# One more V chunk per batch row held in PSUM, with three units between a row's kept passes and an early drain of V

## The chip, the cores and the metric

The kernel runs on one core of one Trainium2 chip. The metric is the time of one execution on the device in microseconds.

## The reference, cut to what matters

A decode step for 8 batch rows: attention over a cache of 4096 positions, 8 key/value heads of 256 elements and 16 query heads, a small MLP block, and then **the same two again with the same caches and weights**.

```python
x = x + _A_ref(_layernorm(x), k_cache, v_cache, wq, wo)    # first pass over the cache
x = x + _B_ref(_layernorm(x), w1, w2, w3, w4)
x = x + _A_ref(_layernorm(x), k_cache, v_cache, wq, wo)    # second pass, same cache
x = x + _B_ref(_layernorm(x), w1, w2, w3, w4)
```

K and V of one row are 32 chunks of 1 MiB, 512 loads for two passes if nothing is kept. A row's second pass needs the row's x from its first pass: its sums, output projection, MLP and new q, called the row's *chain* below.

## The kernel before

The kernel has 15 slots of 1 MiB in SBUF, the on-chip memory that the loads land in. A *unit* is one pass, one row, one pair of heads: 4 K chunks and 4 V chunks. Each row keeps 11 chunks from its first pass to its second, so 8 x 11 = 88 loads are saved and 424 remain. While 11 slots are occupied, the loads of other units go through the remaining four.

```python
NC = 15
kept = [(GP - 1, kv, n) for n in range(4) for kv in range(2)] + [(GP - 2, 0, n) for n in range(3)]
LAG = 4
# order of units, cut: ps 1 is the second pass, keep = pairs 2 and 3, free = pairs 0 and 1
for b in range(Bn):
    tasks += [(1, b, gp) for gp in keep[::-1]]           # second, kept passes of row b
    if b + 1 < Bn:
        tasks += [(0, b + 1, gp) for gp in keep]         # fills the kept slots again
    ...
    tasks += [(1, b, gp) for gp in free]                 # between here and row b+1's kept
    tasks += [(0, b + 2, gp) for gp in free]             # pass: four units, four slots
# V of a unit trails its K by LAG = 4 chunks: K0' V0 K1' V1 ... , also over the kept passes
```

For each K chunk VectorE transposes the slot twice and TensorE forms scores in 32 matmuls; after four chunks ScalarE takes the exponentials, TensorE transposes P, and 16 matmuls per V chunk sum the outputs. The two passes' small matmuls are spread over the units as generators, one step at a time, evenly over a window:

```python
add_gen("chain", b, chain(b, st), idx + 1, first_of[(1, b), 0] - 1, 30)   # from, until, steps
```

The kernel uses eight PSUM banks of 512 words per partition (PSUM is the memory that matmuls sum into): two for scores, three for outputs, one shared (P transposes, spread q, output transposes), two for the chains' sums.

## Time and profile before

The median of the four runs beside the result was 1153.25 us (1149.37 to 1156.13); the profiled execution spanned 1149.6 us. In lines of the profile PE is TensorE, PEld its weight loads, DVE VectorE, ACT ScalarE, POOL GpSimd and SPq the queue from which the loads are issued; L596 is line 596 of the kernel.

| what | value | how to read it |
|---|---|---|
| moved by DMA | 457.52 MB | at 420 GB/s, the best pace seen, 1089.3 us |
| last load landed | 1133 us | last microsecond at over 40 GB/s |
| loss of pace before that | 43.7 us | 1133 - 1089.3 |
| end after it | 16.6 us | 1149.6 - 1133 |

These last two are the booking: span = MB/0.420 + loss + end, the loads' end known to about 1 us. (Expectations of the experiments add up the loss over slices of ten microseconds instead; that gave 42.0 for before.)

### The profile page before, as it was taken

The page shows a single profiled execution, that of the slowest core. Times are in us where ns is not written, and L with a number is a line of the kernel's source. Part 1 is how long each engine was busy: PE and PEld are TensorE (multiplying, and loading weights), DVE is VectorE, ACT ScalarE, POOL GpSimd, SP SyncE. Part 2 cuts the span into 40 slices and gives each one's busy share as a digit, 9 for nine tenths or more (in the row PEclk, how much of TensorE's full clock was granted, in tenths as well). Part 3 has the DMA queues.
Part 4 walks back from the last instruction along what each step waited for, and adds up shares of the span by engine and source line. Part 5 has one row for each costly group of instructions (what it writes and reads, how often), then busy time and mean ns, then how long its engine had stood idle before and what let it go on. Part 6 is the DMA issues. An engine that isn't in the chain of part 4 may idle for free.

```text
span 1149.6 us, 36707 instructions
## 1 busy us (share of the span) xinstructions
PE 705.3 (61%) x17177; PEld 514.0 (45%) x17177; DVE 548.2 (48%) x904; ACT 113.9 (10%) x234; POOL 15.6 (1%) x25
## 2 busy tenths in 40 slices
PE   3144677457755667456764676646665576647787
PEld 2023455345533455344542454425443365425666
DVE  5145453455354544546254553445534553445352
ACT  0001011100110011001110101010011001100100
POOL 0000000000000000000000000000000000000000
PEclk9999997655655556555565557555575556555655
DMA  9999999999999999999999999999999999999993
GB/s 352 375 420 420 407 385 399 418 412 383 414 420 400 385 399 419 420 403 406 409 420 420 400 400 413 420 420 387 402 412 420 408 371 412 420 410 355 410 420 153
DMA packets 68349, 457.52 MB, mean 398 GB/s; under 512 B 6999, under 2 KB 13030, under 8 KB 13542
## 3 DMA queue, kind: packets, MB, share of 16 engines
q1 hardware_dynamic: 68198, 455.19, 98.0%
q8 instruction: 134, 2.20, 0.8%
q14 instruction: 17, 0.14, 0.0%
HBM read 455.15 MB, written 0.01 MB: 396 GB/s over the span
## 4 chain that ended last, share of the span: by engine, by line
DMA 69%; PE 13%; DVE 11%; SPq 3%; issue 2%; POOL 1%; ACT 0%; POOLq 0%; DVEq 0%; ACTq 0%
DMA slot<-in_A_k_cache_dram 62%; DVE slot L547 9%; DMA slot<-in_A_v_cache_dram 6%; PE sc L555 4%; PE o L596 3%; PE y_ps L318 2%; SPq L148 2%; PE q_ps L274 1%; DMA wq_sb<-in_A_wq_dram 1%; SPq L539 1%; PE o L610 1%; DVE qbd L300 1%; PE o L318 1%; PE h_ps L336 0%; PE misc L381 0%
## 5 line engine op out<-in xcount | busy, mean ns | idle before, releaser
L547 DVE STREAM_TRANSPOSE slot<-slot 128x1024 uint32<-128x1024 uint32 x400 | 472.7, 1222 | 383.7 <-DMA slot<-in_A_k_cache_dram 375.0
L555 PE MATMUL sc<-slot,qbd 128*8 128x128 bf16 x8192 | 280.6, 286 | 345.6 <-DVE slot L547 287.2
L555 PEld LDWEIGHTS <-qbd 128*8 128x8 bf16 x8192 | 194.5, 105 | 430.8 <-issue 298.6
L596 PE MATMUL o<-slot,ptw 128*8 128x256 bf16 x3968 | 242.8, 388 | 55.8 <-DMA slot<-in_A_v_cache_dram 33.9
L564 ACT ACTIVATE p_n<-sc 128x512 bf16<-128x512 f32 x64 | 84.7, 1323 | 780.6 <-PE sc L555 780.6
L596 PEld LDWEIGHTS <-ptw 128*8 128x8 bf16 x3968 | 107.9, 109 | 93.8 <-issue 45.0
L318 PEld LDWEIGHTS <-wo_sb 128*128 128x128 bf16 (+1 forms) x1600 | 64.8, 124 | 16.2 <-issue 15.6
L318 PE MATMUL y_ps<-OT,wo_sb 128*128 128x1 bf16 (+1 forms) x1280 | 55.5, 177 | 1.5 <-issue 1.5
L384 DVE RECIPROCAL rz<-misc 128x8 f32<-128x8 f32 (+1 forms) x33 | 6.4, 193 | 96.3 <-PE misc L381 96.3
L274 PEld LDWEIGHTS <-wq_sb 128*128 128x128 bf16 x1152 | 33.9, 104 | 19.1 <-issue 17.3
L274 PE MATMUL q_ps<-xb,wq_sb 128*128 128x1 bf16 (+1 forms) x1152 | 35.3, 166 | 11.4 <-DMA wq_sb<-in_A_wq_dram 3.6
L584 ACT CAST ptw<-misc 128x128 bf16<-128x128 f32 x64 | 17.5, 274 | 211.9 <-PE misc L577 159.4
L411 PEld LDWEIGHTS misc<-R,o_sb 128*128 128x128 f32 x124 | 25.9, 293 | 11.0 <-issue 11.0
L318 PEld LDWEIGHTS <-w_sb 128*128 128x128 bf16 (+1 forms) x630 | 25.7, 125 | 7.3 <-issue 5.2
L411 PE MATMUL misc<-R,o_sb 128*128 128x8 f32 x124 | 28.8, 343 | 0.0
L232 POOL TENSOR_TENSOR t<-t,nhalf 128x2 f32<-128x2 f32 (+1 forms) x17 | 10.7, 630 | 1075.8 <-DVE t L239 978.0
L318 PE MATMUL y_ps<-HT_t,w_sb 128*128 128x1 bf16 (+1 forms) x560 | 24.2, 177 | 0.5 <-DVE HT_t L359 0.5
L300 DVE TENSOR_SCALAR qbd<-misc,quad 128x64 bf16<-128x64 f32 x64 | 13.8, 278 | 22.0 <-PE misc L294 22.0
L381 PE MATMUL misc<-zm,one 128*128 128x8 f32 (+1 forms) x66 | 18.1, 348 | 6.7 <-ACT ptw L584 6.7
L336 PEld LDWEIGHTS <-w_sb 128*128 128x128 bf16 x560 | 17.2, 105 | 9.6 <-issue 9.2
L336 PE MATMUL h_ps<-xb,w_sb 128*128 128x1 bf16 (+1 forms) x560 | 17.9, 166 | 4.9 <-DVE xb L249 4.6
L381 PEld LDWEIGHTS misc<-zm,one 128*128 128x128 f32 x66 | 15.2, 287 | 11.9 <-ACT ptw L584 8.4
(92 smaller groups left out, 207.7 us busy)
## 6 DMA issues: line engine op xcount, KB each, us to landing
slot<-in_A_v_cache_dram SPq DMA_DIRECT2D x224, 1024.0 KB, 12.3
slot<-in_A_k_cache_dram SPq DMA_DIRECT2D x200, 1024.0 KB, 16.4
wo_sb<-in_A_wo_dram SPq DMA_DIRECT2D x1, 3584.0 KB, 26.6
wq_sb<-in_A_wq_dram SPq DMA_DIRECT2D x3, 1024.0 KB, 7.0
w_sb<-in_B_w_dram SPq DMA_DIRECT2D x1, 1568.0 KB, 12.8
w_sb<-in_B_w_dram SPq DMA_DIRECT2D x3, 448.0 KB, 26.8
wq_sb<-in_A_wq_dram SPq DMA_DIRECT2D x2, 256.0 KB, 10.0
w_sb<-in_B_w_dram SPq DMA_DIRECT2D x2, 112.0 KB, 9.0
```

The lines of the kernel that those rows point to most:

```text
L148: nc.sync.dma_start(t[:, fc * cols : (fc + 1) * cols], src[fc * 128 : fc * 128 + 128, :])
L274: nc.tensor.matmul(q_ps[:, j * Hq + h, :], w, xbs(nb)[:, xi, :], start=(fc == 0), stop=(fc == 3),)
L300: nc.vector.tensor_scalar_mul(qbd[:, :, :, a, :], qs.rearrange("p e (f g u h) -> p (e f) u g h", f=2, u=2, h=2)[:, :, u], quad[:, a : a + 1],)
L318: nc.tensor.matmul(r, w[:, i, lo:hi], rhs(i), start=(first and fc == 0 and i == rows[0]), stop=(stop and i == rows[-1]), skip_group_check= ...
L336: nc.tensor.matmul(h_ps[:, c * nb : c * nb + nb], w, xbs(nb)[:, xi, :], start=(fc == 0), stop=(fc == 3),)
L381: nc.tensor.matmul(z_ps, ones, zm[:], start=True, stop=True)
L411: nc.tensor.matmul(ot_ps[:, j], o_sb[:, 128 * j : 128 * j + 128], R[:], start=True, stop=True)
L547: nc.vector.transpose(w, w)
L555: nc.tensor.matmul(sc[32 * k : 32 * k + 8, 128 * x : 128 * x + 128], qbd[:, ep, gp].rearrange("p a h -> p (a h)"), kv[:, k, 2 * half + e2, ...
L564: nc.scalar.activation(p_sb[:].rearrange("p t i x -> p x t i"), sc[:].rearrange("p (x t i) -> p x t i", x=4, t=4), ACT.Exp, scale=scale_ex ...
L584: nc.scalar.copy(ptw[:, :, :, 6:8], pt_ps.rearrange("p t k (a h) -> p a (t k) h", a=4),)
L596: nc.tensor.matmul(o_ps[32 * q : 32 * q + 8, 256 * (g // 4) : 256 * (g // 4) + 256], ptw[:, a, 4 * (y % 4) + y // 4, w : w + 8], v[:, y * ...
```

## The change

Its intent is to save one more load per row. There is no SBUF slot for it, so a chunk of V goes to PSUM through VectorE, as four 32-bit transposes into four banks ("away"), and returns into the slot of the first kept K chunk ("back"). This takes four of the eight banks, so everything else is packed: one bank for scores, with exponentials in halves; two for outputs; the chain's sums in the shared bank.

```diff
-    LAG = 4
+    inner = (GP - 2, 1, 1)
+    sc = psum.tile([128, 512], FP32, name="sc")
+    o_banks = [psum.tile([128, 512], FP32, name=f"o{n}") for n in range(2)]
+    store = [psum.tile([128, 512], FP32, name=f"store{n}") for n in range(4)]
...                                     # the chain's sums now lie in the bank "misc"
+            early = 0 < b < Bn - 3      # order: a unit of row b ahead of the refill
+            tasks += [(1, b, free[0])] * early + [(0, b + 1, gp) for gp in keep]
+            tasks += [(1, b, gp) for gp in free[early : 1 if b == Bn - 3 else 2]]
...
+    def flushed(n):                     # the V of the unit ahead of a second kept pass
+        ...                             # is used before that pass begins
+        return ps == 1 and gp == keep[-1]
...
+    def away(slot):
+        for n in range(4):
+            nc.vector.transpose(
+                store[n][:].bitcast(U32), slot[:].bitcast(U32)[:, 512 * n : 512 * n + 512]
+            )
```

So it has five parts: the chunk in PSUM (eight loads fewer), its moves, the PSUM layout, the order (in four rows three units instead of four between the refill and the kept pass), and the drain of V, called *flush*.

## The prediction

> **What bounds the kernel now.** I read the page first: its tenths by slice, the DMA queue, the chain that ended last. Then I cut the span into stages with the view of busy time by windows, and read the chain of waits in order of time inside one stage.
>
> ```profile
> span 1149.6 us, 36707 instructions
> PE 705.3 (61%) x17177; PEld 514.0 (45%) x17177; DVE 548.2 (48%) x904; ACT 113.9 (10%) x234; POOL 15.6 (1%) x25
> DMA packets 68349, 457.52 MB, mean 398 GB/s; under 512 B 6999, under 2 KB 13030, under 8 KB 13542
> q1 hardware_dynamic: 68198, 455.19, 98.0%
> DMA 69%; PE 13%; DVE 11%; SPq 3%; issue 2%; POOL 1%; ACT 0%; POOLq 0%; DVEq 0%; ACTq 0%
> slot<-in_A_v_cache_dram SPq DMA_DIRECT2D x224, 1024.0 KB, 12.3
> slot<-in_A_k_cache_dram SPq DMA_DIRECT2D x200, 1024.0 KB, 16.4
> ```
>
> The reader is to see that no engine is above 61% while the DMA queue is busy 98%, and that the cache arrives in 424 loads (224 + 200) of 1024 KB. The number 98% hides something: busy is not the same as fast. By windows (after the engines' busy times: granted clock, DMA share, GB/s):
>
> ```profile
> 225.00:296.00 71.00, 46.62 (x1100) 33.70 (x1101) 34.60 (x65) 5.88 (x15) 1.25 (x2) 0.51 1.00 399
> 296.00:353.00 57.00, 34.60 (x832) 23.71 (x831) 26.96 (x30) 6.93 (x14) 0.00 (x0) 0.58 1.01 420
> 353.00:433.00 80.00, 51.02 (x1231) 37.57 (x1232) 39.91 (x74) 7.16 (x15) 1.25 (x2) 0.51 0.99 393
> 433.00:490.00 57.00, 34.70 (x817) 23.70 (x810) 26.85 (x29) 6.96 (x14) 0.00 (x0) 0.57 1.01 420
> 900.00:960.00 60.00, 41.07 (x1008) 31.07 (x1012) 30.32 (x62) 5.21 (x11) 1.25 (x2) 0.50 0.99 387
> 1018.00:1071.00 53.00, 36.43 (x830) 27.11 (x834) 28.89 (x56) 4.84 (x10) 1.25 (x2) 0.50 0.99 377
> 1132.00:1150.00 18.00, 10.80 (x304) 9.65 (x301) 3.89 (x25) 0.21 (x1) 0.70 (x1) 0.50 0.03 9
> ```
>
> Each row of the batch has a stage at 420 GB/s (kept chunks are used up, 15 slots turn over) and a stage at 377 to 405 (11 slots hold kept chunks, only four turn over, and the row's chain of projections and MLP runs among them). In the chain in order of time the second kind looks like this: a load, two transposes, then the next load, with no queue behind it.
>
> ```profile
> 387.65 8.26 DMA slot<-in_A_k_cache_dram
> 395.93 2.38 DVE slot L547 x2
> 399.00 7.16 DMA slot<-in_A_k_cache_dram
> 406.18 2.37 DVE slot L547 x2
> ```
>
> A slot's turn is thus about 7.2 + 2.4 + 0.6 (scores of the second half) + issue = 11 us for K; four slots at 420 GB/s would allow 4 x 2.50 = 10.0.
>
> With 420 GB/s as the pace, the whole span can be booked. 457.52 MB / 420 = 1089.3 us. What is lost in a window is its length x (1 - rate/420): the first 145 us lose 8.7; the eight stages with a chain lose 3.6, 3.6, 5.1, 2.9, 3.2, 4.1, 4.7 and 5.4 = 32.6; the end (from 1071 us) 18.9, of which 17.6 after the last load. Sum 1149.5 against 1149.6 measured. So every megabyte taken away is worth its 2.4 us only as long as the 32.6 do not grow.
>
> **What the Trainium skill says.** "DMA: Bandwidth & Descriptors", Specifications, gives a fabric ceiling of 435 GB/s and about 358 per core from HBM. The trace agrees with the first (420 held for 57 us) and not with the second. The same page's Rules say that a PSUM access by DMA is not possible, hence the round trip through VectorE here. "PSUM — Partial Sum Buffer", PSUM bank collisions raise a hardware error, says two engines may not touch one bank in the same partitions at the same time, even in different columns. In the built instruction order of the changed kernel I see just that: the first scores into a half of the bank wait for the exponentials of the other half. No run yet shows the cost. "VectorE: DVE Perf Modes", The TRN2 errata, puts a fixed 58 cycles on an SBUF source and 120 on a PSUM source at 0.96 GHz. The trace of before has SBUF transposes only: 1204 ns median for 1024 words, which is 1067 ns of stream plus 137 fixed; so the page's 58 cycles (60 ns) is low here.
>
> **The change part by part.**
>
> Removed: one V load for each of eight rows (the built SyncE stream has 429 entries instead of 437). 8 x 1.0486 MB / 420 = 8 x 2.497 = 20.0 us. All eight fall in the second kept pass, whose loads run in the 420 GB/s stage with a queue, so all of it is on the path.
>
> Added on VectorE: four transposes of 128x512 words to PSUM and four back, per row. Each by my estimate 512/0.96 = 533 ns + 0.14 = 0.67 us, up to 0.75 from PSUM: 64 x 0.7 = 45 us over the kernel, 5.6 per row in two lots of 2.8. "Away" falls where the kept slots are being filled: there VectorE is busy 27 of 57 us and landings are up to 21.4 us after the issue, so eight loads are queued and 2.8 us of VectorE time delay nothing. "Back" falls in the second kept pass, where K needs no transposing and VectorE is idle. I count 0 on the path.
>
> Added on ScalarE: exponentials in 128 halves instead of 64 wholes. Half of 1323 ns plus the 268 ns read of the accumulator is about 0.95 us an instruction; the second accumulator reads cost 64 x 0.27 = 17 us more on an engine that is 10% busy. In the four-slot stage K chunks come 5 us apart, so the wait of the third K's scores for the first exponentials is over before its data lands. In the kept pass it costs about 1 us twice.
>
> Moved (flush): the four V chunks of the last unit are used before the kept K chunks. Four V loads in a row land 2.5 us apart; each use frees a slot for the next four loads. When the last V lands, about 10 us of loads are already issued. The first kept K slot handed on comes after 1.1 (last V) + 1.4 (spreading q) + 2 x 1.2 (two scores) = 4.9 us, later ones every 1.2 to 2.2 us. So the queue should not run dry; cost 0 to 0.5 us per row.
>
> Moved (order): four rows have three units (24 loads) instead of four (32) in the four-slot stage. One might take a quarter off the loss. But before contains three-unit stages already: the windows from 225, 900 and 1018 us lose 3.6, 4.7 and 5.4, mean 4.6; the four-unit ones lose 5.1, 2.9, 3.2 and 4.1, mean 3.8. The loss goes with the chain, not with the number of units, and a denser chain loses slightly more. I book 4 x 0.8 = +3 us.
>
> Moved (PSUM): the chain's sums share the bank of the P transposes and of q, so more waits between PE, ScalarE and VectorE; a copy there takes 0.27 us, some three or four per row on the path by estimate: +1 us in all once the ones under DMA waits are left out.
>
> Sum: -20.0 + 3 + 1 = -16 us. From the median of 1155.3: 1139.
>
> **The rivals.**
>
> First: the shorter four-slot stage really pays. Then the loss of the four middle rows falls by a quarter, 15.3 x 0.25 = 4 us, plus sooner freed V slots: 20 + 4 + some = 24 to 28, 1128 to 1131. For it: the author arranged it so, and the loss exists only while four slots turn. Against it: the three-unit stages of before.
>
> Second: the flush or the denser chain starves the queue. The built order puts the last 32 matmuls of the q projection between the last K and the four V chunks. If the row's q or the last probabilities come late, the four V slots come free late, and the DMA queue, which holds only 10 us, empties. 2 us a row would be 16 us and eat the gain: 1150 to 1156. For it: the stage from 1018, the densest, falls to 331 GB/s in one ten-microsecond window. Against it: PE is busy 51 of 80 us in such a stage; with 24 loads and the same chain it would be about 42 of 60, still with room.
>
> Third: VectorE becomes the bound by its added transposes. 548 + 45 = 593 us of 1139 is 52%, and none of it in the stage where slots are short; I hold this for unlikely.
>
> **Range and chances.** The gain of 20 us is certain in bytes, the change of the chain stages is not: between -6 and +9 us. With run-to-run spread (1149.4 to 1156.1 for before) I take 1128 to 1150. A verdict of faster needs about 23 us, more than the removed loads bring alone; it needs the first rival: 0.18. Slower needs a loss of 40 us that nothing in the order suggests: 0.02. Within 2%: 0.80.
>
> **What would show it.** Right: 449.1 MB moved at 420 GB/s in the wide stages, 416 loads, row period shorter by about 2 us (before: 137.0 from 353.78 to 490.76), chain stages that still lose 4 to 5 us per row, the tail after the last load still about 18 us, transposes to and from PSUM of 0.65 to 0.75 us. Wrong in the good direction: chain stages at 405 or more. Wrong in the bad direction: a gap in the loads right after the second kept pass begins, or a queue that drains while VectorE moves the chunk back.

## More of the kernel before

Before and changed kernel were run in turn on the same chip for the result; the experiments ran later beside their own runs of before (medians of 1148 to 1149 us there against 1153 for the result): e1 to e8 on one chip, e9 to e11 on a second and e12 on a third. So experiments are compared by their ratio to the kernel before of the same rounds, or, within e1 to e8, with each other; there the changed kernel was run again as a control.

## The result, and the profile after

The changed kernel took 1136.95 us in the median of four runs (1135.44 to 1140.63) against 1153.25. A ratio here is the mean time of one kernel's runs over that of the other's of the same rounds, so it is not quite the ratio of the medians: 0.9866, with a 95% interval of 0.9823 to 0.9908. The prediction said 1139.

The page after, the same lines as the prediction shows of before:

```profile
span 1134.2 us, 36979 instructions
PE 707.1 (62%) x17177; PEld 518.3 (46%) x17177; DVE 590.9 (52%) x1007; ACT 123.9 (11%) x362; POOL 15.6 (1%) x25
DMA packets 67199, 449.15 MB, mean 396 GB/s; under 512 B 6871, under 2 KB 12902, under 8 KB 13414
q1 hardware_dynamic: 67046, 446.80, 97.2%
PE 4%; DVE 1%; issue 1%; POOL 0%; ACT 0%; POOLq 0%; ACTq 0%
slot<-in_A_v_cache_dram SPq DMA_DIRECT2D x216, 1024.0 KB, 9.9
slot<-in_A_k_cache_dram SPq DMA_DIRECT2D x200, 1024.0 KB, 12.8
```

Eight V loads and 8.37 MB are gone. The mean rate fell from 398 to 396 GB/s, though: some span is not used for loading. The chain that ended last no longer reaches back to any load. It breaks off at 1068 us, where the profile shows no releaser, and everything after that is engines. That is the first sign that the end has changed its bound.

Windows of the same stages, two left out (duration, then busy time of PE, PE's weight loads, DVE, ACT, POOL; granted clock, DMA share, GB/s):

```profile
297.00:368.00 71.00, 41.08 (x1052) 29.78 (x1056) 41.72 (x48) 10.07 (x29) 0.00 (x0) 0.60 1.01 420
368.00:432.00 64.00, 42.77 (x1003) 31.48 (x995) 30.74 (x71) 5.24 (x16) 1.25 (x2) 0.50 0.99 392
890.00:950.00 60.00, 39.74 (x948) 29.31 (x948) 29.11 (x65) 5.03 (x15) 1.25 (x2) 0.50 1.00 398
1010.00:1062.00 52.00, 38.07 (x860) 28.15 (x860) 25.93 (x63) 4.48 (x14) 1.25 (x2) 0.50 0.99 398
1111.00:1134.20 23.20, 16.29 (x449) 14.48 (x445) 4.99 (x31) 1.24 (x4) 0.70 (x1) 0.50 0.01 3
```

The wide stages still hold 420 GB/s, in the one shown with VectorE busy 42 of 71 us (the "away" moves of one row, 2.5 us, lie here). The four-slot stages of the middle rows are shorter (64 us, not 80) at the same rate, and the two late ones improved from 387 and 377 to 398. The last line answers to the 18 us end of before: now 23.2 us without a load. The booking:

| | MB / 0.420 | loss | end | span |
|---|---|---|---|---|
| before | 1089.3 | 43.7 | 16.6 | 1149.6 |
| changed | 1069.4 | 41.6 | 23.2 | 1134.2 |
| difference | -19.9 | -2.1 | +6.6 | -15.4 |

The first column counts bytes, so 19.9 us is what the missing loads can save at most at this pace; what they saved is measured in e3. A third of it was given back at the end. A slot's turn in a four-slot stage, from the VectorE timeline (in brackets: idle time before it and what ended it), is as before, a transpose waiting for each load:

```profile
392.03 2.37 DVE L583 STREAM_TRANSPOSE slot<-slot 128x1024 uint32<-128x1024 uint32 x2 [2.52 <-DMA slot<-in_A_k_cache_dram]
396.99 2.37 DVE L583 STREAM_TRANSPOSE slot<-slot 128x1024 uint32<-128x1024 uint32 x2 [0.32 <-DMA slot<-in_A_k_cache_dram]
```

**Where the end comes from.** The TensorE timeline of before, around the last V chunk of the unit ahead of the last row's kept pass (L596 sums with V, L555 forms scores):

```profile
1072.79 1.03 PE L555 MATMUL sc<-slot,qbd 128*8 128x128 bf16 x32 [1.02 <-DVE qbd L300]
...
1078.07 0.61 PE L596 MATMUL o<-slot,ptw 128*8 128x256 bf16 x16 [0.90 <-DMA slot<-in_A_v_cache_dram]
1078.50 0.66 PE L555 MATMUL sc<-slot,qbd 128*8 128x128 bf16 x32
1080.53 0.61 PE L596 MATMUL o<-slot,ptw 128*8 128x256 bf16 x16 [1.37 <-DMA slot<-in_A_v_cache_dram]
```

The kept scores were slipped between V chunks while TensorE waited for loads: when the last V is used at 1080.5, all four kept K chunks have been. After the change (L646 sums with V, L297 spreads q, L591 forms scores):

```profile
1058.52 1.02 PE L646 MATMUL o<-slot,ptw 128*8 128x256 bf16 x16 [1.46 <-DMA slot<-in_A_v_cache_dram]
...
1059.33 0.32 PE L297 MATMUL misc<-qT,identb 128*32 128x32 bf16 x16
...
1060.67 1.03 PE L591 MATMUL sc<-slot,qbd 128*8 128x128 bf16 x32 [1.02 <-DVE qbd L303]
...
1064.09 1.02 PE L591 MATMUL sc<-slot,qbd 128*8 128x128 bf16 x32 [0.91 <-ACT p_n L600]
...
1066.00 1.02 PE L591 MATMUL sc<-slot,qbd 128*8 128x128 bf16 x32
```

The last V comes first, and then 7.5 us (1059.5 to 1067.0) of spreading q, scores and waits that before lay beside loads. From the use of that last V to the end of the program it is 1149.6 - 1080.5 = 69.1 us before and 1134.2 - 1058.5 = 75.7 after: 6.6 us more, the same as the growth of the end. In this stage TensorE was busy 33.2 of the 39.5 us from 1070.5 to 1110, and the loads still ran at 406 GB/s. That what is put in front of it is added to the time is a reading so far; e1 tests it.

The loads had a gap there too. The issue timeline around it:

```profile
1057.11 0.33 SPq L575 DMA_DIRECT2D slot<-in_A_v_cache_dram  x1
1059.59 7.81 SPq L575 DMA_DIRECT2D slot<-in_A_k_cache_dram  x2
1068.94 0.33 SPq L575 DMA_DIRECT2D slot<-in_A_v_cache_dram  x1
```

Two issues that span 7.81 us: in the last row the first kept slot takes the chunk from PSUM and the next two become scratch memory, so the next load waits for the fourth. The window from 1060 to 1070 us ran at 348 GB/s.

### The profile page after: what moved, and what is told of

Same layout as the page of the kernel before. It is cut to its first block, busy times and chain, and to the rows that moved or that the text cites. A ratio compares the mean times of both kernels' runs of the same rounds, so it can differ in the third digit from the quotient of the medians.

```text
span 1134.2 us, 36979 instructions
## 1 busy us (share of the span) xinstructions
PE 707.1 (62%) x17177; PEld 518.3 (46%) x17177; DVE 590.9 (52%) x1007; ACT 123.9 (11%) x362; POOL 15.6 (1%) x25
## 5 line engine op out<-in xcount | busy, mean ns | idle before, releaser
L591 PE MATMUL sc<-slot,qbd 128*8 128x128 bf16 x8192 | 278.5, 292 | 301.8 <-DVE slot L583 246.3
L591 PEld LDWEIGHTS <-qbd 128*8 128x8 bf16 x8192 | 195.5, 108 | 380.4 <-issue 196.3
L646 PE MATMUL o<-slot,ptw 128*8 128x256 bf16 x3968 | 247.0, 396 | 65.2 <-DMA slot<-in_A_v_cache_dram 45.7
L600 ACT ACTIVATE p_n<-sc 128x256 bf16<-128x256 f32 x128 | 95.4, 746 | 776.6 <-PE sc L591 776.6
L646 PEld LDWEIGHTS <-ptw 128*8 128x8 bf16 x3968 | 111.4, 111 | 111.8 <-issue 61.0
L331 PE MATMUL misc<-OT,wo_sb 128*128 128x1 bf16 (+1 forms) x1280 | 54.1, 176 | 10.1 <-issue 7.9
L277 PEld LDWEIGHTS <-wq_sb 128*128 128x128 bf16 x1152 | 34.9, 104 | 24.6 <-issue 19.2
L277 PE MATMUL misc<-xb,wq_sb 128*128 128x1 bf16 x1024 | 32.3, 165 | 8.2 <-DVE xb L252 4.8
L600 ACT ACTIVATION_READ_ACCUMULATOR p_n<-sc 128x1 f32 x128 | 33.9, 265 | 0.0
L618 DVE STREAM_TRANSPOSE slot<-store 128x512 uint32<-128x512 uint32 x32 | 20.1, 685 | 7.2 <-PE sc L591 7.2
L349 PE MATMUL misc<-xb,w_sb 128*128 128x1 bf16 x504 | 16.1, 165 | 11.0 <-DVE xb L252 9.3
```

Source lines behind the costliest of these rows:

```text
L277: nc.tensor.matmul(q_ps[:, j * Hq + h, :], w, xbs(nb)[:, xi, :], start=(fc == 0), stop=(fc == 3),)
L331: nc.tensor.matmul(r, w[:, i, lo:hi], rhs(i), start=start, stop=stop, skip_group_check=open is not None,)
L349: nc.tensor.matmul(h_ps[:, c * nb : c * nb + nb], w, xbs(nb)[:, xi, :], start=(fc == 0), stop=(fc == 3),)
L591: nc.tensor.matmul(sc[32 * k : 32 * k + 8, 128 * x : 128 * x + 128], qbd[:, ep, gp].rearrange("p a h -> p (a h)"), kv[:, k, 2 * half + e2, ...
L600: nc.scalar.activation(p_sb[:, :, :, 2 * u : 2 * u + 2].rearrange("p t i x -> p x t i"), sc[:, 256 * u : 256 * u + 256].rearrange("p (x t ...
L618: nc.vector.transpose(slot[:].bitcast(U32)[:, 512 * n : 512 * n + 512], store[n][:].bitcast(U32))
```

## The experiments

Theory after the result: the eight loads bring 20 us; the flush costs 6.6 at the end; the rest is near zero. Rivals: the end grew because of the PSUM layout; or the loss of pace, 41.6 for 43.7, hides larger parts of opposite sign. All kernels gave correct results, and none is faster or slower than before by the 2% rule. The profiles' bookings and the runs are in one table:

| run | median us | ratio to before | 95% interval | loss | end |
|---|---|---|---|---|---|
| e1 no flush in the last row | 1131.52 | 0.9863 | 0.9839 to 0.9888 | 40.6 | 18.9 |
| e2 no flush | 1143.31 | 0.9951 | 0.9928 to 0.9974 | 53.6 | 20.1 |
| e3 no chunk in PSUM | 1155.61 | 1.0065 | 1.0044 to 1.0086 | 39.6 | 22.1 |
| e4 before, new order | 1150.85 | 1.0024 | 1.0001 to 1.0047 | 40.7 | 16.7 |
| e5 changed, again | 1138.17 | 0.9910 | 0.9888 to 0.9932 | 41.6 | 23.7 |
| e6 PSUM layout only | 1155.23 | 1.0063 | 1.0034 to 1.0091 | 49.6 | 16.8 |
| e7 before, with flush | 1151.53 | 1.0027 | 0.9998 to 1.0056 | 34.7 | 21.7 |
| e8 changed, old order | 1140.41 | 0.9935 | 0.9911 to 0.9960 | 45.6 | 23.9 |
| e9 flush, chain not spread into it | 1144.33 | 0.9946 | 0.9913 to 0.9979 | 51.6 | 23.2 |
| e10 layout, chain in its own bank | 1152.17 | 1.0012 | 0.9981 to 1.0044 | 44.6 | 17.1 |
| e11 layout, two score banks | 1153.83 | 1.0027 | 0.9996 to 1.0058 | 46.6 | 17.0 |
| e12 e1, chain spread into the flush | 1129.18 | 0.9834 | 0.9808 to 0.9860 | 35.6 | 19.2 |

Loss and end come from one profile each; the two profiles of the changed kernel agree within 0.5 us, but single runs of one kernel differ by up to 11 us (before beside e9: 1145.72 to 1156.60), so a loss is trusted only where the times go the same way. The comparison with the 43.7 of before is the weakest: that execution took 1151.38 us, some 3 us more than the median of before beside the experiments, while the profiled execution of e7, for one, took 1147.64 us, 4 us less than its median. An estimate for the median execution, if the end is the same in every execution, adds to each loss what the median lies above the profiled execution:

| before | changed (e5) | e1 | e2 | e6 | e7 | e9 | e12 |
|---|---|---|---|---|---|---|---|
| 40.8 | 43.3 | 41.5 | 52.0 | 47.2 | 38.6 | 49.9 | 38.8 |

### e1: no flush ahead of the last row

```diff
-        ps, _, gp = tasks[n + 1]
-        return ps == 1 and gp == keep[-1]
+        ps, b, gp = tasks[n + 1]
+        return ps == 1 and gp == keep[-1] and b < Bn - 1
```

> The changed kernel, but without the flush ahead of the last row's second kept pass only (the other rows keep it). Theory: the end after the last load grew from 17.6 to 24.2 us because the flush puts the spreading of q and four kept K chunks (7.7 us of TensorE time in the profile) behind the last V of the unit before, in a stage where TensorE is the bound. Then this kernel ends 5 to 7 us earlier than the changed one: about 1131 us, ratio to before 0.981, and the end after the last load is 17 to 19 us. Rival: the end grew because of the new PSUM layout (exponentials in halves, one scores bank, shared bank for the chain's sums), and the flush has nothing to do with it: then 1137 +- 1.5 us, end 23 to 25 us.

Measured: 1131.52 us, 6.6 below the control e5 in the median, 0.0047 (5.4 us) by ratio. The end is 18.9 us. The last row's flush is what lengthened the end; the layout, which this kernel shares, did not (e6, the layout alone, has an end of 16.8).

### e2: no flush at all

```diff
-        return ps == 1 and gp == keep[-1]
+        return False
```

> The changed kernel without any flush. Theory: in the rows before the last, the flush only moves when V is used and the queue is never empty, so the time is that of the kernel without the last flush, about 1131 us within 2. Rival: the flush frees four V slots ahead of the kept pass and keeps the queue filled there; then this kernel is slower than the one without the last flush by 1 us or more per row, 1138 or more, and the stage after each second kept pass begins below 415 GB/s.

Measured: 1143.31, slower than e1 by 11.8 us in the median (10.1 by ratio) and slower than the changed kernel. The theory that the flush is neutral in the other rows falls. The rival's sign was right, its place was not: the loss of 53.6 us (12 more) lies in the four-slot stages before the kept passes, which ran at 378, 386 and 383 GB/s in the three middle rows, not after them.

### e3: the chunk loaded again

```diff
     def inside(it):
         n, kv, c = it
-        return (tasks[n][2], kv, c) == inner
+        return False
...
-                back(slots[kept_place])
```

> The changed kernel with the eighth V chunk per row loaded again instead of kept in PSUM (no moves to or from PSUM; order, flush and PSUM layout as changed). Theory: eight loads come back, 8 x 2.50 = 20.0 us in the stream of loads; of the last row's 2.5 us most are hidden by the engine-bound end. So 1137 + 17.5 to 20 = 1154.5 to 1157 us. Rival: the 64 transposes (40 us of VectorE) cost time on the path, so leaving them out gives some of it back: then below 1152.

Measured: 1155.61, 17.4 above e5 (17.8 by ratio, known to some 3.5 us). Eight loads are worth about what the bytes say; that the last row's load is partly hidden fits the figure, but these runs do not tell 17.8 from 20. Nothing visible is left for the moves to cost: the loss with and without them is 41.6 and 39.6, no clear difference. It also shows that without the saved loads the other parts together make the kernel slower than before.

### e4: the order alone, in the kernel before

The lines of the order in the diff above, put into the kernel before.

> The kernel before with the changed order of units alone (three instead of four between the kept passes of four rows). Theory of the prediction: a denser chain loses 0.8 us more in each of four rows, 1153 + 3 = 1156. Rival: the shorter stage with four turning slots loses a quarter less, 15.3 x 0.25 = 4 us: 1149. Third: the order moves nothing, 1153 +- 1.

Measured: 1150.85, +0.24% or 2.8 us, with an interval from +0.01 to +0.47%. That is the 3 us booked, as far as it can be told from nothing, and the rival's 4 us gain falls. (The profile's 3 us less loss is no evidence against it: it was the fastest of the six executions, set against a slow one of before.)

### e5: the changed kernel as control

No edit.

> The changed kernel itself, as a control on the chip of the experiments (before took 1148 us beside the first four of them, 1153 beside the prediction). If the kernel without the last flush is really 5 to 7 us faster, this one shows 1136 to 1138 us, ratio 0.990 to 0.992, and an end of 23 to 25 us after the last load; if the two are equal, 1131.5 and 0.986.

Measured: 1138.17, ratio 0.991, end 23.7. So e1's gain is real and the first reading of its ratio (0.9863, equal to that of the result) would have been an accident of comparing two sets of runs of before.

### e6: the PSUM layout alone

The edits of e2 and e3, and the old order.

> The changed kernel with everything undone but its PSUM layout: order of before, no flush, no chunk kept in PSUM; what stays is one bank of scores with exponentials in halves, two banks of outputs, and the chain's sums in the shared bank. New theory, after the run without any flush lost 51.7 us of rate outside the end instead of 40.9: the layout's waits between engines cost some 10 us in the stages with four turning slots, and the flush hides them. Then this kernel is 7 to 11 us slower than before: 1155 to 1159, with 49 to 53 us lost outside the end. Rival: the layout is free, and what the missing flush costs comes from the moves to PSUM or the shorter order: 1148 +- 2, 42 us lost.

Measured: 1155.23, +0.63%, about 7 us (interval 4 to 10), loss 49.6 against 43.7, end unchanged. The layout costs; the rival that called it free falls.

### e7: the flush alone, in the kernel before

The list of items of the changed kernel put in place of the one with LAG = 4, and the condition `n > 0` for the P transposes replaced by `n - 1 in p_of`.

> The kernel before with the flush alone (its order and PSUM layout kept). Theory: the end after the last load grows by 5 to 7 us as in the changed kernel. If the flush relieves only what the new layout costs, the stages stay at 42 us lost and the time is 1153 to 1155. Rival: the flush shortens the loss in the stages by itself, whatever the layout, by 5 to 10 us; then 1144 to 1150, with under 38 us lost outside the end.

Measured: 1151.53, +0.27% (interval from -0.02 to +0.56), between the times of the two. The end grew by 5.1 us to 21.7, as in the changed kernel, so this part of the flush's cost has nothing to do with the layout. The loss fell by 9.0 to 34.7 in the profiles, as the rival said, but the time did not come down to match: with 3 us more time and 5 us more end, the loss fell by about 2 us, give or take 3. The profile was of an execution faster than the median. So whether the flush relieves the stages with the old layout too stays open; with the new layout it does (e2 against e1).

### e8: the old order in the changed kernel

The order of before put back, everything else as changed.

> The changed kernel with the order of before (four units between the kept passes of four rows; flush, store and layout as changed). The order alone in the kernel before moved +0.2% at most. Theory: neutral here too, the changed kernel's time +- 2 us. Rival of the prediction: the shorter stage pays 4 us once the flush is there: 4 us slower than the changed kernel. Prediction's own booking: 3 us faster.

Measured: 1140.41 against 1138.17, ratios 0.9935 and 0.9910 with overlapping intervals; loss 45.6 against 41.6. The sign favours three units once the flush is there, the opposite of e4, but 2 to 3 us are not settled by these runs. The prediction's 3 us in the other direction does not fit.

### e9: why the flush helps

The flush adds four V items ahead of the row's first kept K, and the chain's window ends at that K. So the same 30 steps may be spread over about 20 items instead of 16. This kernel has the flush but ends the window where it would be without:

```diff
-  add_gen("chain", b, chain(b, st), idx + 1, first_of[(1, b), 0] - 1, 30)
+  add_gen("chain", b, chain(b, st), idx + 1, first_of[(1, b), 0] - 5, 30)
```

> The changed kernel with the flush, but the row's chain of projections and MLP spread as if there were none: it ends four items earlier, ahead of the four V chunks of the flush. Theory: the flush recovers 9 to 11 us in the four-slot stages because it gives the chain four more items to spread over (20 instead of 16). Then the loss outside the end goes from 41 back towards 50 us and the time from 1138 to 1144 to 1148. Rival: the recovery comes from something else at the flush (V slots freed without TensorE work between them), and the chain's spread does not matter: 1138 +- 2, loss 40 to 43.

Measured: 1144.33, on another chip than e5 but 6.2 us above it in the median, with no execution of the one among those of the other (1142.60 to 1146.01 against 1135.77 to 1139.01). By ratio it is 0.9946 against 0.9910, 4 us, with intervals that overlap a little, since before ran unevenly in these rounds. The loss in the profile is 51.6, ten more than the changed kernel, but of the slowest of six executions; the estimate above makes it 7 more. The same stages by windows, this kernel first (62, 62 and 61 us long), the changed kernel after it:

```profile
372.00:434.00 62.00, 40.47 (x923) 29.65 (x919) 29.04 (x68) 5.27 (x16) 1.25 (x2) 0.50 0.98 383
508.00:570.00 62.00, 40.42 (x918) 29.35 (x910) 28.96 (x68) 5.27 (x16) 1.26 (x2) 0.50 0.98 381
645.00:706.00 61.00, 40.14 (x918) 29.71 (x922) 29.05 (x68) 5.27 (x16) 1.25 (x2) 0.50 0.98 379
```

```profile
372.00:434.00 62.00, 42.46 (x1000) 31.91 (x1003) 31.29 (x74) 5.97 (x18) 1.25 (x2) 0.50 0.99 391
505.00:565.00 60.00, 40.64 (x946) 29.96 (x942) 29.16 (x69) 5.24 (x16) 1.26 (x2) 0.50 0.99 394
642.00:702.00 60.00, 41.70 (x971) 31.11 (x974) 30.14 (x72) 5.98 (x18) 1.25 (x2) 0.50 0.98 386
```

In the second profile of the changed kernel (e5) the same three windows ran at 394, 397 and 396 GB/s. TensorE is busy two thirds of the time in both kernels, so it is when its work comes that counts. The flush helps in good part because it gives the chain room: 4 to 7 us of the roughly 10 that it is worth in this layout (e2 against e1). The rival, that the spread does not matter, falls; whether the V slots freed without work between them bring the rest is not shown.

### e10 and e11: what in the layout costs

Both start from e6, which has four PSUM banks to spare. e10 gives the chain's sums their own bank, e11 the two halves of the scores a bank each.

```diff
 e10:        if nb == 1:
-            return misc[:, at : at + n]
+            return store[2][:, at : at + n]
```

```diff
 e11: in the scores
-      sc[32 * k : 32 * k + 8, 128 * x : 128 * x + 128],
+      (sc if x < 2 else store[0])[32 * k : 32 * k + 8, 128 * (x % 2) : 128 * (x % 2) + 128],
```

> The kernel of the PSUM layout alone (1155 us, 50.7 us lost outside the end), with the chain's sums of one row in a bank of their own again. Theory: sharing one bank with the P transposes, the spread q and the output transposes makes TensorE, ScalarE and VectorE wait for each other in the four-slot stages; then most of the 8.8 us come back: 1147 to 1150, loss 42 to 45. Rival: the single bank of scores does it; then 1155 +- 2, loss 49 to 52.

> The kernel of the PSUM layout alone, with the two halves of the scores in two banks, so that scores never wait for the exponentials of the other half. Theory: that wait is hidden where K chunks land 5 us apart; 1155 +- 2, loss 49 to 52. Rival: it is what costs; then 1147 to 1150, loss 42 to 45.

Measured: e10 1.0012 (loss 44.6), e11 1.0027 (46.6), against 1.0063 (49.6) for e6. Each seems to give something back, 0.51% and 0.36%, but the intervals of all three overlap, so how the 7 us divide stays open. The traces say where they do not lie: in e6 scores waited for exponentials 11 times, 5.2 us in all, and no such wait lies inside a four-slot stage.

### e12: a version that beats both

e9 showed that a narrower spread costs microseconds, and the flush has room: TensorE stands idle between its V chunks. Part of the changed kernel's TensorE timeline there (L277 is the q projection, the last work of the chain):

```profile
420.50 0.99 PE L277 MATMUL misc<-xb,wq_sb 128*128 128x1 bf16 x32 [0.41 <-ACT ptw L634]
421.42 1.88 PE L646 MATMUL o<-slot,ptw 128*8 128x256 bf16 x32
424.24 1.03 PE L646 MATMUL o<-slot,ptw 128*8 128x256 bf16 x16 [0.93 <-DMA slot<-in_A_v_cache_dram]
428.03 1.02 PE L646 MATMUL o<-slot,ptw 128*8 128x256 bf16 x16 [2.76 <-DMA slot<-in_A_v_cache_dram]
```

So e1 was given a slower pace of the chain in all rows but the last, 26 steps instead of 30 in the window:

```diff
-  ..., first_of[(1, b), 0] - 1, 30)
+  ..., first_of[(1, b), 0] - 1, 30 if b == Bn - 1 else 26)
```

> The best of the runs so far (flush in all rows but the last, 1131.5 us, 40.7 us lost outside the end) with the chain of the other rows paced at 26 steps instead of 30 in its window, so that the q projection falls between the V chunks of the flush, where TensorE waits for loads. Theory from the run with the denser chain (four items fewer cost 10 us of loss): a chain spread wider loses less, by 3 to 6 us: 1126 to 1129, ratio 0.980 to 0.984, loss 35 to 38. Rival: the q projection now delays the last V chunks, hence the slots for the next loads, and the first kept scores; 1131 or slower, loss 41 or more.

Measured: 1129.18 us, ratio 0.9834 (0.9808 to 0.9860), loss 35.6. It is clearly faster than the changed kernel (0.9910) and than before, but that it beats e1 (0.9863, on another chip) by the 3 us of the ratios is not settled: the intervals overlap. The timeline shows the q projection between the V chunks. The waits for V there were 0.93 and 2.76 us in the changed kernel and 0.19 and 1.46 in e1; here the longest is 0.82:

```profile
417.55 1.03 PE L646 MATMUL o<-slot,ptw 128*8 128x256 bf16 x16 [0.82 <-DMA slot<-in_A_v_cache_dram]
418.51 1.87 PE L277 MATMUL misc<-xb,wq_sb 128*128 128x1 bf16 x64
420.31 1.03 PE L646 MATMUL o<-slot,ptw 128*8 128x256 bf16 x16
421.27 1.01 PE L277 MATMUL misc<-xb,wq_sb 128*128 128x1 bf16 x32
422.48 1.02 PE L646 MATMUL o<-slot,ptw 128*8 128x256 bf16 x16 [0.20 <-DMA slot<-in_A_v_cache_dram]
```

## Why the prediction was right or wrong

The predicted time, 1139, and the sum, -16 us, were right to about 2 us of the result (1136.95, or -16.3 by the medians). Part of that is luck, twice over. The working behind the sum was right for the removed loads and the added engine work; the terms that it missed, the flush and the layout, nearly cancelled. And the sum met a base that did not repeat: the changed kernel took 1138.17 us later, but the kernel before 1148.5 instead of 1153.25, and there the gain was 10.3 us (ratio 0.9910, interval 8 to 13 us), 6 less than predicted.

**Removed loads, -20.0.** Right in size: 8.37 MB less, and 17.4 to 17.8 us in the runs (e3), which does not differ clearly from 20. "All of it is on the path" is doubtful for the last row, whose load falls before an end set by engines.

**Added on VectorE, 0 on the path.** The size was right: 692 ns to PSUM and 685 ns from it, for an estimate of 0.67 to 0.75. e3 shows no cost of the moves. That doubling them would be free too was not tried.

```profile
L618 DVE STREAM_TRANSPOSE slot<-store 128x512 uint32<-128x512 uint32 x32 | 20.1, 685 | 7.2 <-PE sc L591 7.2
```

**Added on ScalarE.** Right. The two waits of about 1 us in the kept pass are there (0.91 and 0.85 us in the last row), and in the rows before the last they lie beside loads. "In the four-slot stage [...] the wait [...] is over before its data lands" holds too: of the 17 waits of scores for exponentials in the trace, 11.7 us in all, none lies in a four-slot stage.

**Moved (flush), "cost 0 to 0.5 us per row".** This step failed, in both directions. It looked only at whether the queue runs dry after the flush. It overlooked that the flush moves 7.5 us of spreading q, scores and waits behind the last V, which costs 5 to 7 us ahead of the last row's kept pass, where it is added to the time (e1; the end of e7 grew by 5.1). And it overlooked that the chain is spread over items, so four more items before the kept pass loosen the chain: leaving the flush out costs about 10 us more (e2 against e1), and taking back only the room for the chain 4 to 7 (e9). The queue did run short in one place, the last row, for a reason the working did not see: three kept slots are not handed on there.

**Moved (order), +3.** Right in the kernel before (e4: +2.8 us, barely told from nothing), but not carried over to the changed kernel, where the order of before is not faster but 2 to 3 us slower (e8, not clear of noise). The inference from three stages of before to a cost of 0.8 us per row was drawn from windows that differed in more than their number of units, and none of them had the flush.

**Moved (PSUM), +1.** Mis-sized: the layout alone costs about 7 us (e6). Which of its waits cost them is open (e10, e11).

**What would show it.** "The tail after the last load still about 18 us" was the one check that the result failed at once (23.2), and it led to e1. "Chain stages that still lose 4 to 5 us per row" held for most rows, but as the sum of a layout that added about 6 and a flush that took about 10. Parts measured alone do not add up to the microsecond (the flush takes some 10 us of loss in the new layout and perhaps 2 in the old), so only their signs and rough sizes are claimed.

Of the rivals, the first (a gain of 24 to 28 us) needed the shorter stage to cut the loss; no run shows that it does. e12 gains 19 us against before, with loss and end both lower than in the changed kernel, by other means. The second named the danger at the flush but expected the DMA queue to starve. The third, VectorE as the bound, did not occur: it is busy 52%, as estimated.

Two comparisons with the Trainium skill were read too narrowly. The 358 GB/s of "DMA: Bandwidth & Descriptors" that the trace exceeded are, by that page's section Bandwidth, the share of a core when both cores of its pair stream; this kernel runs on one core only, so nothing here contradicts the page. And the 137 ns found fixed in a VectorE transpose are close to what "VectorE: DVE Perf Modes", The TRN2 errata, itself gives as measured right under its table, about 150 cycles (156 ns at its 0.96 GHz) in place of 58.

## What to carry to other kernels

A load-bound kernel can have places that are not load-bound, here its end: a reordering that is hidden beside loads can be paid in full there, so make exceptions for the last round (0.5% here for one condition). Where side work is spread over a window of a schedule, a change to the window's length is a change of its own, worth 4 to 7 us here where the order and the added engine work showed 3 us or less, so pace the side work on purpose and put its last steps where the engine waits for loads. And when a sum comes out right, check its terms against the profile: here a missed 6 (layout) and a missed 6 (end) stood against a missed gain of about 10 (chain and flush).

## What the Trainium skill lacked or had wrong

- "VectorE: DVE Perf Modes", The three transpose paths: the table sends a VectorE transpose to SBUF only. Here it also wrote PSUM (128x512 32-bit words in 692 ns) and read PSUM (685 ns).
- The TRN2 errata on that page gives 120 cycles (125 ns) for PSUM to SBUF on VectorE. With 533 ns of stream for 512 words at the page's 0.96 GHz, the transpose from PSUM has about 152 ns fixed, and the one to PSUM, for which the table has no column, about 159.
- The same page's errata table has (172 + elements) cycles at 1.2 GHz for ScalarE from PSUM, which makes 357 and 570 ns for 256 and 512 elements. The exponentials here, with strided output and an accumulator, took 746 and 1323 ns, plus 265 ns to read the accumulator.
- No page says what packing into fewer PSUM banks costs a kernel. "PSUM — Partial Sum Buffer" would be the place: here about 7 us of 1150 (e6), of which the runs do not show which waits make it up.
- No page says how many 1 MiB loads a core needs in turn to hold its pace: four slots, each taken for about 11 us by a K load, two transposes and scores, with a row's chain among them, gave 377 to 405 GB/s in the kernel before, and 15 gave 420.
